# Another order of the first loads and steps, and one inverse in two blocks of 16, in a delta-rule attention with two MLPs

## The chip, the cores and the metric

The kernel runs on one core of a Trainium2 chip. The metric is the device time of one execution in microseconds (us), the median of several runs.

## The reference

The first part is a delta rule per batch and head (4 x 8 of them, 768 steps, head dimension 48). Its output goes through two MLPs, the first with a leaky slope alpha per hidden unit, the second with a gate.

```python
k_n = k / (np.linalg.norm(k, axis=-1, keepdims=True) + 1e-06)
for t in range(S):
    y[:, :, t] = np.einsum('bhd,bhde->bhe', q[:, :, t], state)
    v_old = np.einsum('bhde,bhd->bhe', state, kt)
    state = state + bt[:, :, :, None] * np.einsum('bhd,bhe->bhde', kt, vt - v_old)
...
h = x @ w_in
g = np.maximum(h, 0.0) + alpha * np.minimum(h, 0.0)
x = g @ w_out
...
out = (silu(x @ w_gate) * (x @ w_val)) @ w_out
```

x has 3072 rows of 384; the hidden widths are 2048 and 1536. The results are those of fp32.

## The kernel before, in words

The 768 steps are cut into 24 chunks of 32 steps. Within a chunk the recurrence is solved by the inverse of a lower triangular 32 x 32 matrix, one for each of the 32 pairs of batch and head; four chunks make a window, and the 128 inverses of a window lie on the 128 partitions. For a chunk c the steps are: `pre_T` (line 177) transposes k and q on TensorE, `pre_G` (197) multiplies k with k (part 0) and k with q (part 1) and copies them out, the second one with a mask either on VectorE or, with `raw=True`, copied by ScalarE and masked later on GpSimd by `mask_m` (194); `do_KS`, `do_QS`, `do_U`, `do_S`, `do_Y` and `do_XT` (484 to 574) work with the state, apply the inverse, and put the chunk's output into x1, the input of the first MLP. `scale_v` (449) scales v on GpSimd with norms that come out of the inverse. For the first two chunks `pre_cross` (228) replaces the state.

There are two ways to the inverse. `lanes` (313) eliminates 31 rows on VectorE, with the right-hand columns (from 10 on) on GpSimd. `lanes2` (368) treats two diagonal blocks of 16 side by side, 15 steps on VectorE, and gets the block below the diagonal by two products on TensorE for each half of the lanes: `out1` (line 408) and the one at line 430, 64 matmuls each, after each pair a subtraction on VectorE (439). Both are generators; each `next` issues one step. Before the change `lanes2` serves chunks 0 to 3 and `lanes` the rest.

The weights arrive as 64-bit words and are cut to fp32 pairs: `all_w1` (869) is a generator whose step issues ScalarE's scaling (592), one of three VectorE operations (597, 599, 603) and the subtractions on GpSimd and VectorE (875), and for later slices also loads on ScalarE's queue. `load_w1` brings slices of 384 KB; slices 2j and 2j+1 belong to hidden block j, and slices 10 and 11 are thus needed by the first conversion step of block 5, 12 and 13 by that of block 6. Loading k or q of a window is `load_nat` (101): four loads of 192 KB, one for each batch; the even batches fill `nat[0]`, the odd ones `nat[1]`.

The order of work on every engine is the order of the program, written out by hand: `prelude` (910) first, then a list of events `at(u, ...)` sorted by the column u. A column is one hidden block of the first MLP for two chunks: `H1(n, j)` (675, nine matmuls) at 16n + j, its output split by `H1_parts`, and `O1` (705, nine matmuls) 2.5 columns later. H1's results lie in two PSUM banks, so H1 of a column waits until VectorE has read the one two columns before (line 693). The steps of chunk c stand around `base(c)` = 2.9, 7.7, 22.6, 27.2, then 8(c - 2). The conversion goes on up to column 10.5, the inverse of chunks 4 to 7 runs in 37 steps from column 10.9 to 22.6, and `do_U(4)` that needs it stands at 24.1. After the first MLP the second one runs in much the same way.

A small activation that writes one element of a tile makes a later load into that tile wait for ScalarE to come to it; the kernel does so at line 942 for q and at line 987 for the second use of `nat`.

Of the kernel before, what the change touches and what calls it, by code (L numbers as in the profile page):

```python
# [24 lines left out]
def kernel(  # L25
# [25 lines left out]
    nc = tc.nc  # L51
# [49 lines left out]
    def load_nat(w, nm, to, eng=nc.sync):  # L101

        src = {"k": k, "q": q}[nm]
        for b in range(4):
            eng.dma_start(
                out=to[b % 2][:, :, b // 2, 0:D],
                in_=src[b, :, w * 128:w * 128 + 128, :].rearrange("h t d -> t h d"),
            )
# [515 lines left out]
    def load_w1(*slices, eng=nc.sync):  # L624
        for i in slices:
            load_wide(*w1_src(i), w1_64[i // 2][:, i % 2], eng)
# [280 lines left out]

    CONVS = C_A, C_B, C_C, C_D = (1, 3, 3, 1)

    def prelude():  # L910
        nc.vector.memset(St[:, 0, 0:2, :], 0.0)
        for z in range(2):
            nc.vector.memset(nat[z][:, :, :, D:64], 0.0)
        for z in range(2):
            nc.vector.memset(k2_t[z][:, H * D :], 0.0)
        nc.vector.memset(mask[:, 0:1], 1.0)
        nc.scalar.activation(out=mask[:, 1:2], in_=mask[:, 0:1], func=AF.Sqrt)
        make_identity(nc, ident)
        for z in range(2):
            nc.gpsimd.memset(natq0[z][:, :, :, D:64], 0.0)  # L920
        nc.gpsimd.memset(mask, 1.0)
        for g in range(4):
            m = mask[32 * g:32 * g + 32, :]
            nc.gpsimd.affine_select(
                out=m, in_=m, pattern=[[1, C]], compare_op=ALU.is_gt, fill=0.0, base=0, channel_multiplier=-1
            )
        load_nat(0, "k", nat)
        load_w1(0, 1)
        load_beta(0, nc.gpsimd)
        load_v(0, nc.gpsimd)  # L930
        load_v(1, nc.gpsimd)
        warm(4, St[:, 0, 0:2, :].rearrange("p h e -> p (h e)"))
        n = 0
        for b1 in range(2):
            for half in range(2):
                pre_T(0, "k", b1, half, nat, early=n % 2 == 1, eng="act" if n % 2 == 0 else "dve")
                n += 1
        go(conv, 2)
        for c in range(4):
            pre_G(c, (0,), early=c % 2 == 1)  # L940
            if c == 1:
                nc.scalar.activation(out=natq[0:1, 0, 0, 0, 0:1], in_=mask[0:1, 0:1], func=AF.Copy)
        load_nat(0, "q", natq0)
        load_w1(2, 3, 4)
        load_nat(1, "k", nat)
        nc.sync.dma_start(out=alpha_r, in_=moe_alpha.rearrange("(j p) -> j p", p=128))
        load_k2(0)
        load_w1(*range(5, 10))
        go(conv, C_A)
        inv = lanes2(0, True)  # L950
        go(inv, 3)
        load_beta(1)
        n = 0
        for b1 in range(2):
            for half in range(2):
                pre_T(0, "q", b1, half, natq0, early=n % 2 == 1)
                n += 1
        go(inv, 6)
        pre_G(0, (1,))
        go(inv, 2)  # L960
        pre_G(1, (1,), early=True)
        pre_cross()
        for c in (2, 3):
            pre_G(c, (1,), early=c == 2, raw=True)
        pa = bank(False, "pal")
        nc.tensor.transpose(pa[:, 0:J1], alpha_r, ident[0:J1, 0:J1])

        c = slope[:, 0]
        nc.vector.tensor_scalar(c, pa[:, 0:J1], -1.0, 1.0, op0=ALU.mult, op1=ALU.add)
        nc.vector.tensor_scalar(slope[:, 1], c, 0.0, 2.0, op0=ALU.is_ge, op1=ALU.mult)  # L970
        nc.vector.tensor_scalar(slope[:, 1], slope[:, 1], -1.0, None, op0=ALU.add)
        nc.vector.tensor_tensor(c, c, slope[:, 1], ALU.mult)
        nc.vector.tensor_scalar(c, c, -1.0, None, op0=ALU.mult)
        go(inv, 2)
        scale_v(0)
        scale_v(1)
        mask_m(2)
        mask_m(3)
        for b1 in range(2):
            for half in range(2):  # L980
                pre_T(1, "k", b1, half, nat)
        load_k2(1)
        load_w1(*range(10, 2 * W1_SP))
        warm(6)
        go(inv, 7)
        go(inv)
        nc.scalar.activation(out=nat[0][0:1, 0, 0, 0:1], in_=mask[0:1, 0:1], func=AF.Copy)
        load_nat(1, "q", nat)
        go(conv, C_B)
        go(inv)  # L990
        do_U(0)
        load_v(2)
        go(conv, C_C)
        do_KS(1)
        do_QS(0)
        do_Y(0)
        go(conv, 2)
        do_U(1)
        do_QS(1)
        go(conv, 3)  # L1000
        do_XT(0)
        go(conv, C_D)
        do_Y(1)
        go(conv, 1)
        do_XT(1)
        return inv
# [6 lines left out]
    for i in range(CONV_N):  # L1013
        at(-0.5 + i * CONV_END / CONV_N, go, conv)

    for w in range(1, NWIN):
        P = base(4 * w) - 32
        if w == 1:
# [3 lines left out]
                at(1.8 + 1.05 * z, pre_T, 1, "q", z // 2, z % 2, nat)  # L1022
            for z in range(4):
                at((5.7, 7.0, 8.8, 10.4)[z], pre_G, 4 + z)
            l0, l1, n = 10.9, 22.6, LANES
        else:
            if w < TURN:
                at(P - 5, load_nat, w, "k", nat)
# [121 lines left out]
```

## Time and profile before

| | |
|---|---|
| runs (us) | 1096.22, 1096.61, 1093.04; median 1096.22 |
| profiled execution | 1096.7 us, of it 1094.7 us from the first to the last instruction |
| busy, share of the span | TensorE 96%, VectorE 56%, ScalarE 35%, GpSimd 32% |
| granted TensorE clock | 0.976 in the mean |

In the rows further down, PE is TensorE's matmuls, PEld its weight loads, DVE VectorE, ACT ScalarE, POOL GpSimd, SP the queue that issues most loads; PEclk is the granted TensorE clock, 1.00 being 2.4 GHz and 0.50 being 1.2 GHz. Times count from the start of the span. A square bracket tells how long the engine was idle before and what released it; "issue" is a wait for nothing that the profile shows. An fp32 matmul of the attention part is recorded twice, so the 64 matmuls of a product are 128 records, while H1 and O1 are nine records each. The ends of matmuls are modelled and overlap with the next.

### The profile page before, as it was taken

What the parts mean: (1) busy time and instruction counts of PE and PEld (TensorE: products, weight loads), DVE (VectorE), ACT (ScalarE), POOL (GpSimd) and SP (SyncE); (2) the same over time, 40 slices, a digit from 0 to 9 for tenths busy, and PEclk for the clock granted to TensorE, in tenths of its full rate; (3) what the DMA queues carried; (4) which work ended last, traced back from release to release, by engine and by line L of the source; (5) the groups of instructions that cost most, each with busy time, mean ns of one, the idle gap of its engine ahead of it and who ended that gap; (6) DMA issues with size and microseconds to landing.
All of it is one profiled execution on the core that took longest, in us unless ns stands there. A gap on an engine that the chain in (4) does not pass through costs nothing.

```text
span 1094.7 us, 35682 instructions
## 1 busy us (share of the span) xinstructions
PE 1054.4 (96%) x15661; PEld 969.7 (89%) x15661; DVE 610.8 (56%) x1218; ACT 387.7 (35%) x833; POOL 346.2 (32%) x517
## 2 busy tenths in 40 slices
PE   5688899999999999999999999999999999999998
PEld 5578888999999999999999998888888888888887
DVE  5689974985796598589443453433333333333332
ACT  3356343344334434443444653222122222222211
POOL 4275652843573283266333541201001001010000
PEclk8569999999999999999999999999999999999999
DMA  8674051453345236330341441010010010100001
GB/s 180 179 203 113 10 100 47 71 112 104 68 57 145 67 62 137 90 85 10 118 128 57 153 137 58 1 58 1 1 58 1 16 43 1 58 1 1 29 1 29
DMA packets 165979, 76.34 MB, mean 70 GB/s; under 512 B 129824, under 2 KB 160576, under 8 KB 165824
## 3 DMA queue, kind: packets, MB, share of 16 engines
q1 hardware_dynamic: 160256, 66.28, 24.6%
q10 hardware_dynamic: 5184, 7.37, 2.1%
q8 instruction: 122, 2.00, 0.8%
q0 software_dynamic: 384, 0.41, 0.2%
q14 instruction: 33, 0.27, 0.1%
HBM read 57.52 MB, written 16.52 MB: 68 GB/s over the span
## 4 chain that ended last, share of the span: by engine, by line
PE 91%; DVE 5%; issue 2%; DMA 1%; ACT 1%; SPq 0%; ACTq 0%; DVEq 0%
PE gv L772 27%; PE o L713 19%; PE h L682 18%; PE o L802 14%; PE pst L527 2%; PE pg L207 2%; PE pu L506 2%; PE py L548 2%; PE pk L462 2%; PE py L462 1%; PE pt L185 1%; PE px L570 1%; DVE X L331 1%; DVE tmp L323 1%; DVE w L599 0%
## 5 line engine op out<-in xcount | busy, mean ns | idle before, releaser
L772 PE MATMUL gv<-x2s,w 128*128 128x512 f32 x1296 | 307.6, 391 | 0.0
L772 PEld LDWEIGHTS gv<-x2s,w 128*128 128x128 f32 x1296 | 242.5, 188 | 47.7
L713 PE MATMUL o<-gh,w 128*128 128x256 f32 x1728 | 245.6, 288 | 3.5 <-POOL gh L702 1.8
L682 PE MATMUL h<-xh,w 128*128 128x256 f32 x1152 | 240.7, 285 | 4.0 <-DVE pn L693 2.9
L702 POOL TENSOR_TENSOR gh<-pn,gh 128x256 fp32r<-128x256 f32 x192 | 157.0, 817 | 250.3 <-ACT gh L701 224.3
L713 PEld LDWEIGHTS o<-gh,w 128*128 128x128 f32 x1728 | 217.2, 189 | 9.5 <-POOL gh L702 2.4
L682 PEld LDWEIGHTS h<-xh,w 128*128 128x128 f32 x1152 | 191.4, 190 | 7.3 <-DVE pn L693 4.4
L693 DVE SCALAR_TENSOR_TENSOR pn<-pn,slope,h 128x256 f32<-128x256 f32 x192 | 91.2, 475 | 132.9 <-ACT pn L692 132.8
L682 PE MATMUL h<-xl,w 128*128 128x256 f32 x576 | 162.8, 283 | 0.1
L802 PE MATMUL o<-w,us 128*128 128x384 f32 x864 | 162.5, 337 | 0.0
L802 PEld LDWEIGHTS o<-w,us 128*128 128x128 f32 x864 | 151.9, 188 | 7.1 <-DVE os L815 1.3
L692 ACT ACTIVATE pn<-h,slope 128x256 f32<-128x256 f32 x192 | 90.2, 470 | 139.9 <-PE h L682 139.6
L784 DVE TENSOR_TENSOR sg<-sg,gv 128x512 f32<-128x512 f32 x72 | 49.5, 687 | 152.2 <-ACT sg L782 152.1
L701 ACT ACTIVATE gh<-pn 128x256 fp32r<-128x256 f32 x192 | 79.9, 416 | 142.0 <-DVE pn L693 140.2
L682 PEld LDWEIGHTS h<-xl,w 128*128 128x128 f32 x576 | 109.4, 190 | 0.6 <-DVE xl L574 0.6
L789 ACT ACTIVATE us<-u 128x512 fp32r<-128x512 f32 x72 | 45.5, 632 | 171.1 <-DVE u L785 171.1
L757 POOL TENSOR_TENSOR x2s<-x2r,x2s 128x512 fp32r<-128x512 f32 x15 | 19.3, 1310 | 266.6 <-ACT x2s L755 266.6
L782 ACT ACTIVATE sg<-gv 128x512 f32<-128x512 f32 x72 | 43.0, 597 | 159.4 <-PE gv L772 159.4
L790 DVE TENSOR_TENSOR us<-u,us 128x512 fp32r<-128x512 f32 x72 | 49.9, 693 | 54.5 <-ACT us L789 54.5
L785 DVE TENSOR_TENSOR u<-sg,gv 128x512 f32<-128x512 f32 x72 | 49.5, 687 | 49.3 <-PE gv L772 48.8
L331 DVE TENSOR_TENSOR X<-X,tmp 128x31 f32<-128x31 f32 (+29 forms) x155 | 65.1, 420 | 4.8
L323 DVE TENSOR_TENSOR tmp<-L,X 128x31 f32<-128x31 f32 (+29 forms) x155 | 57.8, 373 | 1.8
(121 smaller groups left out, 970.5 us busy)
## 6 DMA issues: line engine op xcount, KB each, us to landing
w<-in_moe_w_out_dram SPq DMA_DIRECT2D x19, 384.0 KB
wf<-w2d SPq DMA_DIRECT2D x36, 192.0 KB
k<-in_k_dram SPq DMA_DIRECT2D x96, 48.0 KB
x2d<-xs SPq DMA_DIRECT2D x12, 384.0 KB
w<-in_moe_w_gate_dram SPq DMA_DIRECT2D x12, 384.0 KB
w<-in_moe_w_val_dram SPq DMA_DIRECT2D x12, 384.0 KB
x2r<-x2d SPq DMA_DIRECT2D x24, 192.0 KB
v<-in_v_dram SPq DMA_DIRECT2D x88, 48.0 KB
```

The lines of the kernel that those rows point to most:

```text
L323: eng.tensor_tensor(w, t.L[:, i + 1:C, i:i + 1].to_broadcast([128, n, m]), t.X[:, i:i + 1, c0:c0 + m].to_broadcast([128, n, m]), ALU.mult,)
L331: eng.tensor_tensor(Xv, Xv, w, ALU.subtract)
L682: nc.tensor.matmul(ps[:, 0:N1], w[:, a, kk * 128:kk * 128 + 128], x[b][:, kk, :], start=(i == 0), stop=(i == 3 * NK - 1),)
L692: nc.scalar.activation(out=g, in_=hv, func=AF.Relu, scale=slope[:, 0, j:j + 1])
L693: nc.vector.scalar_tensor_tensor(out=g, in0=g, scalar=slope[:, 1, j:j + 1], in1=hv, op0=ALU.mult, op1=ALU.add)
L701: nc.scalar.activation(out=gh[:, 0], in_=g, func=AF.Copy)
L702: nc.gpsimd.tensor_tensor(gh[:, 1], g, gh[:, 0], ALU.subtract)
L713: nc.tensor.matmul(o[:, dm // 2, (dm % 2) * N1:(dm % 2) * N1 + N1], w[:, a, dm * 128:dm * 128 + 128], g[:, b], start=(j == 0 and i == 0 an ...
L772: nc.tensor.matmul(p[:, 0:N2], w2[j, z][:, a, kk * 128:kk * 128 + 128], x[:, b, kk], start=(i == 0), stop=(i == 3 * NK - 1),)
L784: nc.vector.tensor_tensor(sg, sg, ps[0], ALU.mult)
L790: nc.vector.tensor_tensor(us[:, 1], u, us[:, 0], ALU.subtract)
L802: nc.tensor.matmul(o2_t[n][t][:, 0:DM], us[:, a, t * 128:t * 128 + 128], w[:, b, :], start=(j == 0 and i == 0), stop=(j == J2 - 1 and i == 2),
```

## The change

The prelude is put into another order. The four loads of `load_nat` go in the order of batches 0, 2, 1, 3. SP's first loads become q of window 0, k of window 1, alpha, w1 slices 2 to 5, k of chunk 0, w1 slices 6 to 9, k of chunk 1; slices 10 and 11 wait for a mark behind the first product of the inverse, and q of window 1, slices 12 and 13 and v of chunk 2 for one behind `do_Y(0)`. The steps of the first inverse go on without other VectorE work between them: the masks of chunks 0 and 1 go to GpSimd behind the 17 steps, as does `scale_v`; alpha is copied by ScalarE, and the slopes are worked out behind `do_XT(0)`. The six warm matmuls are gone. `pre_G` of chunks 2 and 3 and their masks leave the prelude for columns 4.3 to 10.2. The inverse of chunks 4 to 7 is made by `lanes2`: 21 steps from column 10.9 at a distance of 0.33 and four from 19.4 at a distance of 0.7, so that the four products stand at 17.5, 19.4, 20.1 and 20.8.

```diff
     def load_nat(w, nm, to, eng=nc.sync):
...
-        for b in range(4):
+        for b in BS:
...
+    def mark(a):
+        nc.scalar.activation(out=a, in_=mask[0:1, 0:1], func=AF.Copy)
...
         load_nat(0, "q", natq0)
-        load_w1(2, 3, 4)
         load_nat(1, "k", nat)
         nc.sync.dma_start(out=alpha_r, in_=moe_alpha.rearrange("(j p) -> j p", p=128))
+        load_w1(*range(2, 6))
         load_k2(0)
-        load_w1(*range(5, 10))
+        load_w1(*range(6, 10))
+        load_k2(1)
...
-        go(inv, 6)
-        pre_G(0, (1,))
-        go(inv, 2)
-        pre_G(1, (1,), early=True)
+        pre_G(0, (1,), raw=True)
+        pre_G(1, (1,), early=True, raw=True)
         pre_cross()
-        for c in (2, 3):
-            pre_G(c, (1,), early=c == 2, raw=True)
-        pa = bank(False, "pal")
+        pa = bank(True, "pal")
         nc.tensor.transpose(pa[:, 0:J1], alpha_r, ident[0:J1, 0:J1])
...
+        nc.scalar.activation(out=slope[:, 1], in_=pa[:, 0:J1], func=AF.Copy)
         for b1 in range(2):
             for half in range(2):
                 pre_T(1, "k", b1, half, nat)
-        load_k2(1)
-        load_w1(*range(10, 2 * W1_SP))
-        warm(6)
-        go(inv, 7)
+        go(inv, 17)
+        for c in range(2):
+            scale_v(c)
+        for c in range(2):
+            mask_m(c)
         go(inv)
-        nc.scalar.activation(out=nat[0][0:1, 0, 0, 0:1], in_=mask[0:1, 0:1], func=AF.Copy)
-        load_nat(1, "q", nat)
+        mark(w1_64[5].rearrange("p a n -> p (a n)").bitcast(F32)[0:1, 0:1])
+        load_w1(10, 11)
         go(conv, C_B)
         go(inv)
         do_U(0)
-        load_v(2)
         go(conv, C_C)
         do_KS(1)
         do_QS(0)
         do_Y(0)
+        mark(nat[0][0:1, 0, 0, 0:1])
+        load_nat(1, "q", nat)
+        load_w1(*range(12, 2 * W1_SP))
+        load_v(2)
         go(conv, 2)
...
         do_XT(0)
+        c = slope[:, 0]
+        nc.vector.tensor_scalar(c, slope[:, 1], -1.0, 1.0, op0=ALU.mult, op1=ALU.add)
...
+    def step1(box):
+        if not box:
+            box.append(lanes2(1))
+        go(box[0])
...
-            l0, l1, n = 10.9, 22.6, LANES
+            for z in range(2):
+                at((4.3, 9.6)[z], lambda z=z: pre_G(2 + z, (1,), raw=True))
+                at((4.9, 10.2)[z], mask_m, 2 + z)
+            n = 0
+            box1 = []
+            for z in range(LANES2 - 4):
+                at(10.9 + 0.33 * z, step1, box1)
+            for z in range(4):
+                at(19.4 + 0.7 * z, step1, box1)
```

## Rows read from the trace of the kernel before

**Rows 1.** The stages: stretch, busy us of each engine (records), PEclk, DMA share, GB/s

```profile
0.00:60.60 60.60, 36.80 (x1291) 32.90 (x1291) 37.19 (x85) 24.28 (x52) 25.06 (x40) 0.68 0.74 176
...
91.30:116.80 25.50, 22.66 (x677) 20.34 (x676) 24.75 (x34) 13.51 (x26) 14.25 (x12) 1.00 0.30 77
116.80:149.40 32.60, 27.79 (x269) 25.21 (x267) 30.64 (x81) 10.85 (x32) 24.77 (x54) 1.00 0.23 46
...
200.00:1094.70 894.70, 889.42 (x11324) 818.76 (x11322) 462.73 (x918) 299.89 (x636) 244.76 (x373) 1.00 0.23 59
```

**Rows 2.** TensorE in order of time, prelude: start us, us, line, tiles, records [idle before]

```profile
25.93 0.53 PE L235 MATMUL pg<-kqt 48*32 48x64 f32 x10 [2.61 <-issue]
...
38.05 1.53 PE L408 MATMUL pi<-TT,GL 32*32 32x16 f32 x128 [2.06 <-DVE TT L273]
...
44.80 0.83 PE L430 MATMUL pi<-tmp,Dm 16*32 16x16 f32 x44 [3.34 <-issue]
46.14 1.50 PE L506 MATMUL pu<-v,TT 32*32 32x48 f32 x64 [0.51 <-DVE TT L439]
...
60.62 0.58 PE L682 MATMUL h<-xh,w 128*128 128x256 f32 x1 [1.07 <-ACT xh L573]
```

**Rows 3.** VectorE in order of time, prelude

```profile
20.21 0.20 DVE L392 TENSOR_TENSOR tmp<-L,X 128x30 f32<-128x30 f32 x1
...
23.01 0.78 DVE L392 TENSOR_TENSOR tmp<-L,X 128x110 f32<-128x110 f32 x1
...
30.98 0.17 DVE L969 TENSOR_SCALAR slope<-pal 128x16 f32<-128x16 f32 x1 [5.05 <-PE pal L966]
...
36.95 1.05 DVE L273 STREAM_TRANSPOSE TT<-X 128x512 f32<-128x512 f32 x1
...
60.60 0.56 DVE L574 TENSOR_TENSOR xl<-px,xh 128x384 fp32r<-128x384 f32 x1 [0.65 <-ACT xh L573]
```

**Rows 4.** VectorE groups, 19.4 to 37 us: busy us, mean ns, idle before

```profile
L394 DVE TENSOR_TENSOR X<-X,tmp 128x30 f32<-128x30 f32 (+7 forms) x15 | 4.4, 293 | 0.4
```

**Rows 5.** Matmul records from the start up to a stop (x)

```profile
0.00:98.70 98.70, 71.70 (x2260) 0.74 0.74 186
0.00:103.99 103.99, 75.33 (x2388) 0.75 0.71 178
```

**Rows 6.** TensorE in order of time, 93 to 105 us

```profile
94.98 0.97 PE L207 MATMUL pg<-kqt 48*32 48x64 f32 x51 [0.82 <-issue]
...
100.36 0.85 PE L713 MATMUL o<-gh,w 128*128 128x256 f32 x5 [1.65 <-issue]
...
104.36 0.37 PE L462 MATMUL py<-St,kqt 48*32 48x48 f32 x14 [0.37 <-issue]
```

**Rows 7.** SP, TensorE and ScalarE in order of time: loads and who reads them

```profile
12.60 2.65 SPq L105 DMA_DIRECT2D natq<-in_q_dram  x4
...
17.19 3.81 PE L185 MATMUL pt<-ident,natq 128*128 128x128 f32 x16 [1.92 <-DMA natq<-in_q_dram]
...
58.49 0.91 ACT L592 ACTIVATE w<-w 128x768 f32<-128x768 f32 x1
```

**Rows 8.** H1's matmuls (line 682) in columns 11 to 21: stretch, busy us (records)

```profile
113.80:149.36 35.56, 14.33 (x99) 12.29 (x100) 1.00 0.20 42
```

**Rows 9.** TensorE in order of time, in the loop

```profile
69.03 1.42 PE L408 MATMUL pi<-TT,GL 32*32 32x16 f32 x128
...
89.14 1.10 PE L207 MATMUL pg<-kqt 48*32 48x64 f32 x64
...
143.14 1.31 PE L713 MATMUL o<-gh,w 128*128 128x256 f32 x9
...
145.36 0.60 PE L185 MATMUL pt<-ident,nat 128*128 128x128 f32 x4
```

**Rows 10.** VectorE groups, 116 to 156 us

```profile
L331 DVE TENSOR_TENSOR X<-X,tmp 128x60 f32<-128x60 f32 (+29 forms) x31 | 12.4, 401 | 1.0
```

More of the change, by code (lines that the diff above doesn't have):

```diff
@@ L941, in prelude @@
             if c == 1:
-                nc.scalar.activation(out=natq[0:1, 0, 0, 0, 0:1], in_=mask[0:1, 0:1], func=AF.Copy)
+                mark(natq[0:1, 0, 0, 0, 0:1])
         load_nat(0, "q", natq0)
-        load_w1(2, 3, 4)
         load_nat(1, "k", nat)
         nc.sync.dma_start(out=alpha_r, in_=moe_alpha.rearrange("(j p) -> j p", p=128))
+        load_w1(*range(2, 6))
         load_k2(0)
-        load_w1(*range(5, 10))
+        load_w1(*range(6, 10))
+        load_k2(1)
         go(conv, C_A)
@@ L957, in prelude @@
                 n += 1
-        go(inv, 6)
-        pre_G(0, (1,))
-        go(inv, 2)
-        pre_G(1, (1,), early=True)
+        pre_G(0, (1,), raw=True)
+        pre_G(1, (1,), early=True, raw=True)
         pre_cross()
-        for c in (2, 3):
-            pre_G(c, (1,), early=c == 2, raw=True)
-        pa = bank(False, "pal")
+        pa = bank(True, "pal")
         nc.tensor.transpose(pa[:, 0:J1], alpha_r, ident[0:J1, 0:J1])
[L968 to L978, printed above, removed]
+        nc.scalar.activation(out=slope[:, 1], in_=pa[:, 0:J1], func=AF.Copy)
         for b1 in range(2):
@@ L1001, in prelude @@
         do_XT(0)
+        c = slope[:, 0]
+        nc.vector.tensor_scalar(c, slope[:, 1], -1.0, 1.0, op0=ALU.mult, op1=ALU.add)
+        nc.vector.tensor_scalar(slope[:, 1], c, 0.0, 2.0, op0=ALU.is_ge, op1=ALU.mult)
+        nc.vector.tensor_scalar(slope[:, 1], slope[:, 1], -1.0, None, op0=ALU.add)
+        nc.vector.tensor_tensor(c, c, slope[:, 1], ALU.mult)
+        nc.vector.tensor_scalar(c, c, -1.0, None, op0=ALU.mult)
         go(conv, C_D)
```

## The prediction

> **What bounds the kernel now.** I read the stages first [rows 1]. From 200 us to the end TensorE is busy 889.4 of 894.7 us at full clock, so a change of the first 200 us passes to the end one for one, unless it adds or removes TensorE work. Before 60.6 us TensorE works 36.8 us, at a mean clock of 0.68: this is the prelude, and what ends it is a chain of waits. Between 116.8 and 149.4 us it works 27.8 of 32.6 us while VectorE is busy 30.6: there the elimination of chunks 4 to 7 holds it. Between 91.3 and 116.8 us VectorE is busy 24.8 of 25.5: the weight conversion holds it.
>
> Next, TensorE in the prelude [rows 2]: the products of the first inverse start at 38.05, the second product stops for 3.34 us that nothing in the profile explains ("issue"), `do_U(0)` starts at 46.14 and the first H1 at 60.62. Then VectorE [rows 3, 4]: the elimination starts at 20.21, stands still for 5.05 us until the transpose of alpha is done, works off the slopes, and ends at 36.95. Its 30 instructions, 15 on X as in [rows 4] and 15 on tmp (4.2 us), are busy 8.6 us of these 16.7.
>
> The "issue" stops have a pattern [rows 5, 6]. Two of them fall after 2260 and 2388 matmul records, 128 apart, in the middle of groups whose data are there. So every 128 records (a small fp32 matmul counts as two) there is a border, and from border 2260, left at 100.36, to the release of 2388 at 104.36 it took 4.0 us. I read this as a supply of instructions in blocks: 128 records of small matmuls last about 1.4 us, of H1 and O1 some 15 us (18 records in 2.22), so only crowds of small matmuls can outrun it.
>
> **The change, term by term**, against the profiled execution's 1096.7 us.
>
> *A, up to do_U(0).* The new order of the four loads of k (0, 2, 1, 3) lets the first transposes start after two loads instead of three; q, at 17.19, waits 4.5 us after the first issue for three of its four [rows 7]. With about 1.1 us per load I take 1.0 us for all that follows (0 if the fourth load or ScalarE's sqrt sets the pace, 1.5 at best). The slopes leave the elimination, the two masks go to GpSimd, and scale_v comes after it: in its time one VectorE step took 0.78 us where the mean is 0.29 [rows 3, 4]. Left are 8.6 us of work and 0.7 of gaps, less some 0.5 of that slowdown: 8.9 us for 16.74, so −7.85. The first product starts at 38.05 − 1.0 − 7.85 = 29.2. TensorE must be free by then: the cross products, at 25.93 behind a border [rows 2], end 1.0 earlier near 25.5; alpha and the 16 transposes of k, like q's 3.8 us at half clock [rows 7], follow: 29.3. It is just free. The stretch from this product to do_U(0) was 8.1 us with the 3.34 us stop. The border there now waits 1.7 us by 4.2 us per block, as w1 slices 10 to 13 no longer load beside it; then the subtraction also has three conversion steps ahead of it on VectorE. I take 6.6, so −1.5. Sum A: −10.3 (−7 if TensorE comes 2 us late and the stop stays; −11 at best).
>
> *B, do_U(0) to the first H1:* 14.5 us before. VectorE now works off the slopes (five small instructions from 30.98, about 1.3 us) behind do_XT(0), and it was idle only 0.65 us before the last xl [rows 3]: +0.7. Slices 12 and 13 of w1 now wait, on SP's queue, behind four loads of q that start only with the mark behind do_Y(0). The mark comes near 41.7. The four q loads went out in 2.65 us and three of them were in 4.5 us after the first issue [rows 7]; the fourth and 0.77 MB of weights bring this to about 8 us, 49.7. ScalarE needs the slices for the conversion that stood at 58.49, 12.35 us behind do_U(0) [rows 7]; that is 48.2 now. Behind that instruction on ScalarE's queue stands the copy that H1 waits for. +1.3 (0 to 3, as ScalarE's own weight loads share the engines). Queued behind them on SP is v of chunk 2; its reader comes over 10 us later, free. alpha and k2(1) are on SP ahead of their readers, free. ScalarE gets five more small copies (two G, alpha, two marks); it is busy 24.3 of 60.6 us [rows 1], which hides them, and without that cover they cost some 1.5. Sum B: +2.0; the first H1 comes 8.3 us earlier, at 52.3.
>
> *C, in the loop, columns 0 to 11.* G of chunks 2 and 3 (64 records each) come out of the prelude. One such group takes 1.1 us [rows 9] (at 89.14), half a border comes with it. At column 4.3 TensorE has no slack: +1.6. At 9.6 VectorE sets the pace: +0.5 (0 to 1.6). Their masks, two GpSimd steps, slow VectorE's conversion: +0.3 (0 to 0.8). Sum C: +2.4. The six warm matmuls that go stood in idle time: nothing, unless they kept the clock up; it fell again before the second product.
>
> *D, the inverse.* Columns 11 to 22 (99 H1 records) last 35.6 us [rows 8]. O1 and H1 of a column take 2.22 us [rows 9] (143.14 to 145.36), eleven columns 24.4; with S and Y (64 records each, priced like the G at 89.14) 2.0, and with 19 full-width records of XT and four transposes at 0.12 another 2.3, that is 28.7. So 6.9 us are lost to VectorE, more than the 4.8 idle of [rows 1], since pipelined tails count as busy. VectorE's elimination there takes 23.1 us in 31 steps (12.4 on X as in [rows 10], 10.7 on tmp), 0.75 a step and 3.16 steps a column, beside pn. Two blocks take 15 steps of about 0.59: three a column and pn make 2.2 us, just TensorE's pace. The three transposes, 3 us, fall near column 17.3, where the new product gives cover. −6.5 (−4.8 to −6.9). TensorE gets four products of 128 records, 1.42 us each with the changeover [rows 9] (at 69.03): +5.7 (6.5 at half clock). These 512 records bring four borders; the products at 19.4, 20.1 and 20.8 stand 0.7 columns (1.6 us) apart, so 128 records pass in 2.7 us and the supply needs 4.0 [rows 6]: 1.1 to 1.3 us short at two of them, none at the others. +2.2 (0 to 8). Sum D: +1.4.
>
> Sum: −10.3 + 2.0 + 2.4 + 1.4 = −4.5, so 1092.2. The profiled execution lies 0.5 us above the median of the runs (1096.2), so I forecast 1091.7 for the median. Where the clock rises behind the first H1 shifts with its start; nine H1 records take 2.2 us instead of 1.1 at half clock, so 1.5 either way for that.
>
> A rule speaks to the last term of D. The Trainium skill (Runtime: NRT & Kernel Launch, "Instruction fetch mechanics") says that instructions come in 16 KiB blocks of 256 and that crossing into the next is mostly hidden. The trace agrees on the size (128 records, each a weight load and a matmul) and disagrees on hidden wherever small matmuls crowd. By that rule D would be −0.8 and the whole about 1089.
>
> **The rivals.**
> *1. Borders are mostly free* (the page's rule): 2.2 us less in D and 0.5 in C, 1089.0. For it: most borders in the trace pass without a stop. Against it: the stops of [rows 6]. 0.12.
> *2. The prelude gives only 6.* If the loads of w1 slices 12 and 13 take 3 us too long, or TensorE reaches the products 2 us late, A and B make −5.5 instead of −8.3 and the whole ends at 1094.5: no change. For it: TensorE is free only just in time, and ScalarE's queue is strict. Against it: fewer bytes compete. 0.25.
> *3. Slower: the products starve.* Between column 17.5 and do_QS(4) at 22.95 some 760 records pass, six blocks. At the 5.4 us from one release at 94.98 to the next at 100.36 [rows 6] they need 32 us where the work takes 21: 11 us instead of 2.2, so 1100.5. It decides from about 5 us a block. For it: the q loads of chunks 8 to 11 and the weight loads run there. Against it: the very next block took 4.0, and DMA is light there (0.23 before 149.4 [rows 1]). 0.15.
> The change does what it says: the order of each engine is written out by hand, so I give no chance to its not being carried out.
>
> **How the numbers follow.** Forecast and what lies close, 1088.5 to 1094.5: 0.48; rivals as above. Faster by over 0.3% (under 1092.9; 0.3% is about what a measurement of this kernel can tell): 0.42 of the forecast and rival 1, 0.54. Within 0.3%: rival 2 and 0.05 of the forecast, 0.30. Slower: rival 3 and rest, 0.16. The range takes in rival 1 with its best A and rival 2 with half a clock slip, and stops short of rival 3: 1086.5 to 1098.
>
> **What would show it.** Right: VectorE's 30 elimination steps without a stop of 5 us, first product near 29, do_U(0) near 36, first H1 near 52; on ScalarE a wait of 1 to 2 us on w1 near 48; no pn wait on TensorE in columns 13 to 20, and "issue" stops of about 1 us within the products of columns 20 and 21. Wrong: a first H1 after 55, stops of 2 us or more in the products, or VectorE still the pace between columns 13 and 20.

## The result and the profile after

The changed kernel took 1102.91 us (median of six runs, 1102.21 to 1105.6) against 1096.23 for the kernel before beside it. The measured ratio, which is not the quotient of these two medians, is 1.0073, interval 1.0059 to 1.0087. By the medians it is slower by 6.7 us, where 4.5 less were forecast; the range ended at 1098.0. The profiled execution spans 1101.4 us (1094.7 before). All executions of a kernel here lie within about one per cent of its median, but for one of run 9's ten, of 1725 us, which its ratio leaves out.

First the stages of the kernel after, as in [rows 1] and [rows 8] (stretch, busy us of each engine with its records, PEclk, DMA share, GB/s; the last row of H1's matmuls alone, columns 11 to 21):

```profile
0.00:58.40 58.40, 34.11 (x1152) 29.61 (x1152) 35.75 (x83) 23.99 (x54) 24.23 (x40) 0.67 0.79 184
...
116.80:149.40 32.60, 26.68 (x597) 25.52 (x584) 21.31 (x61) 10.67 (x29) 8.24 (x12) 0.95 0.18 39
...
200.00:1101.40 901.40, 896.30 (x11438) 825.68 (x11436) 468.53 (x941) 303.22 (x644) 249.03 (x381) 1.00 0.23 59
...
111.56:156.92 45.36, 15.30 (x99) 13.66 (x100) 0.92 0.23 51
```

From 116.8 to 149.4 us VectorE is busy 21.3 us where it was 30.6: the relief is there. TensorE is busy 1.1 us less than before, though it has more to do. H1's columns 11 to 21 last 45.4 us where they lasted 35.6, at a mean clock of 0.92. The loss sits here: the first H1 still starts 2.2 us earlier than before, column 28 starts 7.5 us later, and what follows is as long as it was (921.9 us, 922.6 before).

TensorE of the kernel after in order of time, in the prelude, against [rows 2]:

```profile
26.91 0.58 PE L235 MATMUL pg<-kqt 48*32 48x64 f32 x11 [2.98 <-issue]
...
30.87 0.99 PE L408 MATMUL pi<-TT,GL 32*32 32x16 f32 x97
33.57 0.47 PE L408 MATMUL pi<-TT,GL 32*32 32x16 f32 x31 [1.70 <-issue]
34.56 1.48 PE L430 MATMUL pi<-tmp,Dm 16*32 16x16 f32 x97 [0.53 <-issue]
38.15 0.62 PE L430 MATMUL pi<-tmp,Dm 16*32 16x16 f32 x31 [2.10 <-issue]
39.35 1.50 PE L506 MATMUL pu<-v,TT 32*32 32x48 f32 x64 [0.58 <-POOL w L875]
...
58.37 0.58 PE L682 MATMUL h<-xh,w 128*128 128x256 f32 x1 [2.81 <-ACT xh L573]
```

The first product starts 7.2 us earlier, do_U(0) 6.8 and the first H1 2.25. Next VectorE, against [rows 3]: the elimination runs from 20.18 to 28.94, 8.76 us without the stop of 5 us.

```profile
20.18 0.20 DVE L392 TENSOR_TENSOR tmp<-L,X 128x30 f32<-128x30 f32 x1
...
28.94 1.09 DVE L273 STREAM_TRANSPOSE TT<-X 128x512 f32<-128x512 f32 x1
```

ScalarE in order of time (ACTq is its own queue for loads), with SP's loads of q:

```profile
45.45 2.72 SPq L105 DMA_DIRECT2D nat<-in_q_dram  x4
48.22 2.14 SPq L608 DMA_DIRECT2D w<-in_moe_w_in_dram  x1
...
53.65 0.36 ACTq L608 DMA_DIRECT2D w<-in_moe_w_out_dram  x1
54.11 0.49 ACT L557 ACTIVATE ys<-py 128x384 f32<-128x384 f32 x1 [4.02 <-DMA nat<-in_q_dram]
56.28 0.88 ACT L592 ACTIVATE w<-w 128x768 f32<-128x768 f32 x1 [1.69 <-DMA w<-in_moe_w_out_dram]
```

ScalarE stands 4.02 us for a load of q that it does not read: in the trace the fourth load of q, issued at 47.40, and ScalarE's weight load of 53.65, the instruction ahead, complete on the same semaphore, number 101, and the weight load waits for it. Then it stands 1.69 us for the weights. The copy that H1 waits for is behind both.

TensorE in the loop, columns 17 to 21, against [rows 9], then VectorE at the same place:

```profile
135.41 1.43 PE L408 MATMUL pi<-TT,GL 32*32 32x16 f32 x128 [4.16 <-DVE TT L273]
136.77 2.29 PE L713 MATMUL o<-gh,w 128*128 128x256 f32 x9
...
148.71 0.59 PE L408 MATMUL pi<-TT,GL 32*32 32x16 f32 x48 [0.95 <-issue]
...
152.53 0.70 PE L430 MATMUL pi<-tmp,Dm 16*32 16x16 f32 x62 [0.91 <-issue]
...
155.15 1.94 PE L713 MATMUL o<-gh,w 128*128 128x256 f32 x9
```

```profile
133.71 0.19 DVE L394 TENSOR_TENSOR X<-X,tmp 128x30 f32<-128x30 f32 x1
133.81 0.47 DVE L693 SCALAR_TENSOR_TENSOR pn<-pn,slope,h 128x256 f32<-128x256 f32 x1
134.21 1.05 DVE L273 STREAM_TRANSPOSE TT<-X 128x512 f32<-128x512 f32 x1
```

The first product, at column 17.5 in TensorE's order, stands 4.16 us for VectorE, whose elimination ends only at 133.9. Behind it O1 takes 2.29 us instead of 1.3, and again behind the stops of the last product (1.94). The stages say what the clock was:

```profile
131.00:135.40 4.40, 0.25 (x3) 0.04 (x2) 4.16 (x13) 1.78 (x5) 1.84 (x3) 1.00 0.00 2
135.40:138.80 3.40, 3.39 (x137) 3.36 (x138) 1.65 (x2) 0.39 (x1) 0.15 (x1) 0.62 0.02 5
...
150.80:157.00 6.20, 5.29 (x149) 5.09 (x148) 0.90 (x2) 0.98 (x3) 1.54 (x3) 0.72 0.74 160
```

### The profile page after: what moved, and what is told of

Read it like the earlier page. It is cut to its first block, busy times and chain, and to the rows that moved or that the text cites. A ratio compares the mean times of both kernels' runs of the same rounds, so it can differ in the third digit from the quotient of the medians.

```text
span 1101.4 us, 36626 instructions
## 1 busy us (share of the span) xinstructions
PE 1059.1 (96%) x16161; PEld 975.1 (89%) x16161; DVE 596.3 (54%) x1186; ACT 389.5 (35%) x839; POOL 331.9 (30%) x478
## 4 chain that ended last, share of the span: by engine, by line
PE 90%; DVE 5%; issue 2%; DMA 1%; SPq 1%; ACT 0%; POOL 0%; ACTq 0%; POOLq 0%; DVEq 0%
PE gv L772 27%; PE o L713 19%; PE h L682 18%; PE o L802 14%; PE pst L527 2%; PE pg L207 2%; PE pu L506 2%; PE py L548 2%; PE pk L462 2%; PE py L462 1%; PE pt L185 1%; DVE X L394 1%; DVE tmp L392 1%; PE px L570 1%; DVE w L599 1%
## 5 line engine op out<-in xcount | busy, mean ns | idle before, releaser
L785 DVE TENSOR_TENSOR u<-sg,gv 128x512 f32<-128x512 f32 x72 | 49.5, 687 | 49.7 <-PE gv L772 48.8
L331 DVE TENSOR_TENSOR X<-X,tmp 128x60 f32<-128x60 f32 (+29 forms) x124 | 52.6, 424 | 3.9
L323 DVE TENSOR_TENSOR tmp<-L,X 128x60 f32<-128x60 f32 (+29 forms) x124 | 46.8, 377 | 1.2
```

Of the source, the lines that this page charges most:

```text
L331: eng.tensor_tensor(Xv, Xv, w, ALU.subtract)
L785: nc.vector.tensor_tensor(u, sg, ps[1], ALU.mult)
```

## The experiments

The table has the median of each run, its ratio to the kernel before beside it, and from TensorE's rows the start of do_U(0) and of H1 in columns 0, 11 and 28.

| run | us | ratio, interval | do_U(0) | col. 0 | col. 11 | col. 28 |
|---|---|---|---|---|---|---|
| before | 1096.23 | | 46.14 | 60.62 | 113.80 | 172.06 |
| after | 1102.91 | 1.0073, 1.0059 to 1.0087 | 39.35 | 58.37 | 111.56 | 179.51 |
| 1 prelude only | 1095.31 | 0.9999, 0.9987 to 1.0011 | 38.94 | 58.28 | 112.87 | 171.58 |
| 2 inverse only | 1103.64 | 1.0072, 1.0055 to 1.0088 | 46.75 | 60.63 | 110.32 | 180.96 |
| 3 first product late | 1101.95 | 1.0061, 1.0041 to 1.0080 | 39.34 | 58.72 | 111.65 | 177.18 |
| 4 loads early | 1102.65 | 1.0070, 1.0051 to 1.0089 | 38.93 | 56.96 | 112.88 | 182.09 |
| 5 no products | 1091.81 | 0.9962, 0.9947 to 0.9976 | 38.57 | 58.33 | 111.05 | 167.76 |
| 6 products apart | 1100.91 | 1.0046, 1.0032 to 1.0060 | 41.51 | 60.97 | 115.27 | 177.66 |
| 7 q last | 1096.20 | 1.0003, 0.9992 to 1.0014 | 38.44 | 56.13 | 112.80 | 171.41 |
| 8 G in idle time | 1094.17 | 0.9988, 0.9975 to 1.0000 | 39.01 | 58.73 | 111.12 | 171.77 |
| 9 weights late | 1102.45 | 1.0051, 1.0031 to 1.0072 | 37.15 | 56.30 | 109.11 | 175.40 |
| 10 loads in turn | 1102.18 | 1.0061, 1.0039 to 1.0082 | 39.45 | 59.12 | 112.98 | 178.81 |
| 11 warm | 1094.64 | 0.9982, 0.9966 to 0.9999 | 38.30 | 58.08 | 109.84 | 170.83 |
| 12 longer elimination | 1094.21 | 0.9980, 0.9964 to 0.9997 | 39.67 | 59.07 | 109.47 | 171.43 |
| 13 masks early | 1094.47 | 0.9976, 0.9962 to 0.9991 | 38.53 | 57.58 | 107.04 | 167.87 |
| 14 all three | 1096.10 | 0.9988, 0.9973 to 1.0003 | 38.85 | 58.69 | 109.93 | 170.93 |
| 15 masks early, weights late | 1094.87 | 0.9994, 0.9983 to 1.0005 | 37.30 | 58.37 | 110.48 | 170.96 |

One profile's columns 0 to 10 differ by 1.6 to 3.5 us between kernels that are alike up to there (after and runs 3, 5 and 6: 52.7 to 54.3; run 2 and before: 49.7 and 53.2), so single profiles are compared column by column and totals by the medians. A profile can also lie off its kernel's median: run 13's was the fastest of its twelve executions (1090.5 us), run 9's the fastest of its ten (1099.1).

**Runs 1 and 2: each half of the change alone.**

```diff
-            n = 0
-            box1 = []
-            for z in range(LANES2 - 4):
-                at(10.9 + 0.33 * z, step1, box1)
-            for z in range(4):
-                at(19.4 + 0.7 * z, step1, box1)
+            l0, l1, n = 10.9, 22.6, LANES
```

Run 1 is the kernel after with this; run 2 is the kernel before with the reverse.

> The changed kernel with the inverse of chunks 4 to 7 put back to the 37 elimination steps of before; prelude and G of chunks 2 and 3 as changed. Theory (the loss sits in the inverse's products, columns 16 to 22, where the changed kernel is 9.9 us longer than the one before; the prelude still gains 2.2): first H1 at 58.4, columns 16 to 22 in about 20.3 us as before, the whole 1093.5 to 1094.5, faster than before by 2 us. Rival (the new prelude moves the loop into a worse position of instruction borders and clock, whatever inverse runs): columns 16 to 22 stay over 25 us and the whole stays above 1098.

> The kernel before with only the inverse of chunks 4 to 7 in two blocks, at the same columns as in the changed kernel. Theory: columns 16 to 22 in about 30 us against 20.3, a wait of about 4 us of TensorE for VectorE's transpose ahead of the first product, the whole 1104 to 1106, slower than the changed kernel by its prelude's 2 us. Rival (the inverse costs only its product work, 5.6 us, less VectorE's relief): 1097 to 1099.

The inverse alone costs what the whole change costs (1.0072), and the new prelude alone changes nothing (0.9999): I had expected some 2 us of gain to be left, and run 2 to be slower than the kernel after by as much. So the loss is the inverse's own, and it does not come from the earlier prelude: run 2 has the same wait (TensorE's waits from 110 to 180 us: who waited for whom, us in total, times, longest).

```profile
PE pi L408 <- DVE TT L273: 4.2, 1, 4.2
```

**Run 3: the first product at 19.4 instead of 17.5.**

```diff
-            for z in range(LANES2 - 4):
+            for z in range(LANES2 - 5):
                 at(10.9 + 0.33 * z, step1, box1)
-            for z in range(4):
+            for z in range(5):
                 at(19.4 + 0.7 * z, step1, box1)
```

> The changed kernel with the first of the four products moved from column 17.5 to 19.4, and the other three, 0.7 columns apart, behind it (20.1, 20.8, 21.5). Theory: VectorE comes to the transpose that the first product reads about 4 us after TensorE stands there; two columns later it is there, so the wait of 4.2 us goes, and with it the half clock behind it (about 1.5 us). The whole 1096.5 to 1098. Rival (the wait moves with the product, or the products' own work and borders are the loss): gain under 2 us, 1101 or more.

The wait is gone and the total all but stays: a miss for my theory, and the rival's 1101 or more. TensorE of run 3 in order of time:

```profile
145.97 0.69 PE L408 MATMUL pi<-TT,GL 32*32 32x16 f32 x60 [0.47 <-issue]
...
150.25 1.15 PE L430 MATMUL pi<-tmp,Dm 16*32 16x16 f32 x69 [1.73 <-issue]
151.32 2.29 PE L713 MATMUL o<-gh,w 128*128 128x256 f32 x9
```

With the products closer to each other a block's border stops one for 1.73 us, and O1 behind it runs at half clock again. Taking the wait away moves part of its cost into stops; the rest must be in the products themselves. Runs 5 and 6 price them.

**Run 5: no products; run 6: products 1.3 columns apart.**

```diff
             ps[z] = bank(early, "pi")
+            if w == 1:
+                nc.tensor.matmul(ps[z][:, 0:N], ident, G[:, 0:HC, 0:HC], start=True, stop=True)
+                return
```

Run 5 is run 3 with this and the same for the second product: it leaves the products out and puts one wide matmul in the place of each. Run 6 is run 3 with

```diff
-                at(19.4 + 0.7 * z, step1, box1)
+                at((18.6, 19.9, 21.2, 22.5, 23.0)[z], step1, box1)
```

> The third run's kernel (first product at column 19.4), in which the four small products of the second inverse (512 small matmuls, 1024 records) are left out: one wide matmul fills each of the four halves of a PSUM bank in their place, so the output is not the reference's. It prices the small products with their borders and the half clock behind them against the third run, and the relief of VectorE alone against the first run. Theory (the products cost about 5.2 us of work, 2.2 of stops and some 2 of half clock; the relief of VectorE is smaller than the 6.5 us I counted, near 3.5): 1093 to 1094.5, columns 16 to 22 in 17 to 19 us. Rival (the relief is the whole 6.5 us, so the products cost 12): 1089 to 1091. Second rival (there is no relief, TensorE had the time anyway): 1095 to 1097.

> The kernel after, with the twenty steps up to the end of the elimination as they are and the four products at columns 18.6, 19.9, 21.2 and 22.5, 1.3 columns (2.9 us) apart instead of 0.7. Theory (supply: a block of 128 records takes about 4 us, so products that stand closer stop, and the stops pull the clock down): the stops within the products go, the clock stays up to column 22, 1097 to 1099. Rival (the products cost their work and break the clock wherever they stand, since 16x16 matmuls leave most of TensorE empty): 1101 to 1103, H1 at half clock behind each product.

Run 5 is 10.1 us faster than run 3 and 3.5 faster than run 1, better than my theory's 1093, short of the rival's whole relief. In run 6 the clock stays at 1.00 in every stretch from column 16 to 28, as the theory had it, and yet the total is 1100.9, above its 1097 to 1099. Columns 16 to 27 of run 6, then of run 5 (stages), and what run 6 waits for in order of time on TensorE:

```profile
130.42:177.66 47.24, 43.62 (x1275) 41.20 (x1275) 20.54 (x47) 19.40 (x52) 12.54 (x17) 1.00 0.33 74
```

```profile
126.18:167.76 41.58, 39.84 (x772) 37.67 (x772) 20.41 (x47) 19.44 (x52) 12.57 (x17) 1.00 0.37 83
```

```profile
139.16 1.25 PE L408 MATMUL pi<-TT,GL 32*32 32x16 f32 x128 [1.49 <-DVE TT L273]
...
153.87 0.93 PE L430 MATMUL pi<-tmp,Dm 16*32 16x16 f32 x88 [0.66 <-issue]
...
157.60 0.57 PE L462 MATMUL pk<-St,kqt 48*32 48x48 f32 x33 [1.08 <-issue]
```

The 5.66 us between the two are, but for 0.2, four products at 1.2 (4.8, less 1.2 for run 5's four wide matmuls) and 3.6 us in which TensorE is idle, against 1.7 in run 5. So with full clock and hardly a stop the products still cost their work, and that work alone is about what VectorE's relief is worth. The medians of the two runs differ by 9.1 us, 3.4 more than these columns show; for that no stage gives a cause.

**Runs 4, 7 and 10: the loads.** Run 4 is the kernel after with

```diff
-        load_w1(10, 11)
+        load_w1(*range(10, 2 * W1_SP))
+        mark(nat[0][0:1, 0, 0, 0:1])
+        load_nat(1, "q", nat)
...
-        mark(nat[0][0:1, 0, 0, 0:1])
-        load_nat(1, "q", nat)
-        load_w1(*range(12, 2 * W1_SP))
```

Run 7 is run 1 with the longer `load_w1` of this edit, and with the mark and the load of q behind do_XT(1) instead. Run 10 is the kernel after with the old order of the loads:

```diff
-        for b in BS:
+        for b in range(4):
             eng.dma_start(
```

> The changed kernel with q of window 1 and w1 slices 12 and 13 loaded behind slices 10 and 11, ahead of do_U(0), as before the change. Theory (ScalarE stands 4.0 us in its own weight load, which waits until a load of q has landed, and 1.7 us for slices 12 and 13): both waits go; the first H1 comes at 53 to 55 instead of 58.4, the whole 1098 to 1100. Rival (the heavier loads ahead of do_U(0) hold up TensorE's instruction blocks there): do_U(0) comes 2 us or more later and the first H1 still after 57.

> The first run's kernel (prelude of the kernel after, inverse of the second window as before), with w1 slices 12 and 13 loaded right behind slices 10 and 11, and the four loads of q for chunks 4 to 7 moved to the end of the prelude, so that no q load shares a completion semaphore with ScalarE's own weight load. Theory (ScalarE's stand of 4 us in the kernel after came from the q loads issued just ahead): ScalarE no longer waits, first H1 near 55, 1092.5 to 1094.5 if the columns behind keep their pace. Rival (as in the fourth run, what ScalarE wins is lost to slower instruction blocks under the weight loads): first H1 at 57 or later, 1095 to 1096.

> The kernel after with the four loads of k and q of each window in their old order 0, 1, 2, 3. I had counted 1.0 us for the new order. Theory (the second half of the transposes waits for the fourth load at 7.7 us in either order, so the order is worth nothing): do_U(0) at 38.5 to 40, 1102 to 1104, no difference from the kernel after. Rival (the order gives its 1.0 us, hidden by a block's border that fell elsewhere): do_U(0) one later, near 40.3, 1103.5 to 1105.

In run 4 both waits of ScalarE are gone, and the first H1 comes only 1.4 us earlier, as the stops in TensorE's small matmuls grew: neither the theory's 53 to 55 nor the rival's later do_U(0). In run 7 the first H1 starts at 56.1, near the theory, but column 11 at 112.8, as in run 1, and the total is that of before: a miss for the theory, and not by its rival's way. Its gain is gone by column 3 (74.30; 74.11 in run 1): ScalarE now stands 4.16 us at 67.19 for a load of k, and in the columns 0 to 2 TensorE is busy 17.4 of 18.2 us at a mean clock of 0.53. Run 10 cannot be told from the kernel after: the order of the loads is worth nothing that these runs can tell.

**Run 9: fewer bytes beside the products.**

```diff
         load_k2(0)
-        load_w1(*range(6, 10))
         load_k2(1)
...
-        mark(w1_64[5].rearrange("p a n -> p (a n)").bitcast(F32)[0:1, 0:1])
-        load_w1(10, 11)
         go(conv, C_B)
         go(inv)
+        for z in (3, 4, 5):
+            mark(w1_64[z].rearrange("p a n -> p (a n)").bitcast(F32)[0:1, 0:1])
+        load_w1(*range(6, 12))
         do_U(0)
```

> The kernel after with w1 slices 6 to 11 loaded only behind the second product of the first inverse, just ahead of do_U(0), so that few bytes move while the elimination's last part and the two products run. Read in the prelude alone: do_U(0) at 38.4 to 41.5 us in the seven profiles with the order of after, with 4.3 us of stops inside the first two products in the kernel after. Theory (an instruction block takes longer to come while the weights load): the stops in the two products fall to 1.5 to 2.5 us, do_U(0) near 36.5 to 37.5; the weights then come late, first H1 at 58 or later, total 1102 to 1105. Rival (a block takes its 4 us whatever the loads do): stops of 4 us again, do_U(0) at 38.5 to 40.

Stages from 28 to 38 us (the last numbers are clock, DMA share and GB/s) of the kernel after, of run 4 and of run 9:

```profile
28.00:38.00 10.00, 5.81 (x241) 5.38 (x239) 6.23 (x10) 5.64 (x15) 4.52 (x6) 0.67 0.68 202
```

```profile
28.00:38.00 10.00, 4.16 (x250) 3.50 (x252) 5.33 (x6) 4.32 (x10) 5.69 (x7) 0.67 0.74 196
```

```profile
28.00:38.00 10.00, 7.36 (x315) 6.79 (x317) 7.21 (x11) 5.75 (x17) 5.72 (x7) 0.67 0.20 39
```

The stops in the first two products sum to 4.33 us at a DMA share of 0.68, 5.74 at 0.74 and 1.79 at 0.20. TensorE of run 4, then of run 9, their longest:

```profile
37.73 0.62 PE L430 MATMUL pi<-tmp,Dm 16*32 16x16 f32 x31 [3.21 <-issue]
```

```profile
35.69 0.62 PE L430 MATMUL pi<-tmp,Dm 16*32 16x16 f32 x31 [1.25 <-issue]
```

Same product, same 97 records ahead of the border: the instruction block comes later while the weights load. How much later does not go by the share alone: in the thirteen profiles that load these weights here, at shares of 0.61 to 0.74, the stops sum to anything from 3.2 to 6.4 us. do_U(0) came as the theory had it, the first H1 earlier (56.3, where 58 or later was expected). That a prelude 2 us shorter moves the total little (1102.45) belongs to the next group.

**Runs 8, 11 to 15: where the prelude's gain goes.** Run 8 is run 1 with G of chunks 2 and 3 behind the prelude's last transposes; run 13 adds their masks:

```diff
-            for z in range(2):
-                at((4.3, 9.6)[z], lambda z=z: pre_G(2 + z, (1,), raw=True))
-                at((4.9, 10.2)[z], mask_m, 2 + z)
...
         do_XT(1)
+        for c in (2, 3):
+            pre_G(c, (1,), early=c == 2, raw=True)
+        for c in (2, 3):
+            mask_m(c)
```

Runs 11 and 12 are run 8 with the first and the second of these; run 14 is run 13 with both, and run 15 is run 13 with run 9's edit.

```diff
         do_Y(1)
+        warm(8)
...
             pre_G(c, (1,), early=c == 2, raw=True)
+        warm(4)
```

```diff
-            l0, l1, n = 10.9, 22.6, LANES
+            l0, l1, n = 10.9, 23.4, LANES
```

> The first run's kernel with G of chunks 2 and 3 issued behind the last transposes of the prelude, where TensorE waits 2.8 us for ScalarE, instead of at columns 4.3 and 9.6. It prices part C of the change. Theory (each group costs 1.1 us of work and half a border in the loop): columns 0 to 11 shorter by about 2.4 us, first H1 later by at most 0.5, 1093 to 1094. Rival (TensorE had slack in columns 0 to 11, since the weight conversion on VectorE paces them): no change, 1095 to 1096.

> The eighth run's kernel (prelude of after, inverse as before, G of chunks 2 and 3 behind the prelude) with 12 wide matmuls without use set into TensorE's idle time before the first H1: eight behind do_Y(1), four behind G. In all profiles so far the columns 0 to 3 begin at half clock and H1 of column 6 starts at 88.5 to 90.7 us whether the first H1 starts at 56.1 or at 60.6 (one at 93.1). Theory (what an earlier first H1 wins is lost since the clock then rises no earlier): with TensorE kept busy the clock is up by the first or second column, column 6 starts near 86.5, 1091 to 1092.5. Rival (the conversion of the weights and its loads pace the columns up to 9): the clock rises earlier, TensorE waits more, column 9 as before, 1093.5 to 1095.

> The eighth run's kernel with the steps of the second window's elimination (as before, without products) spread over columns 10.9 to 23.4 instead of 22.6, to see whether VectorE's relief is to be had by spreading alone. Theory (VectorE is short by some 3 us in these columns, and 0.8 column more gives it 1.8): 1092.5 to 1093.8. Rival (the inverse is then late for do_U(4) at column 24.1 and TensorE waits there): 1094.5 to 1097.

> The eighth run's kernel with the masks of chunks 2 and 3 on GpSimd right behind their G at the end of the prelude, instead of at columns 4.9 and 10.2. In the eighth run do_Y(3) stood 3.28 us at 117.96 for GpSimd's second mask, which sits behind the last conversion step on GpSimd's queue. Theory (this wait is what C's move still cost, and the prelude's gain was lost there): the wait goes, H1 of column 14 near 122 instead of 124.9, 1091 to 1092.5. Rival (VectorE's conversion, whose last step ended at 116.3 with G moved as without, paces these columns): the wait goes and pn waits and waits for U take its place, 1093.5 to 1094.5.

> The thirteenth run's kernel with the 12 wide matmuls of the eleventh run and the elimination spread to column 23.4 as in the twelfth, the parts that were not slower each, together. Theory: 1090.5 to 1092.5. Rival (they draw on the same slack): 1093 to 1094.5.

> The thirteenth run's kernel with w1 slices 6 to 11 loaded behind the second product of the first inverse, as in the ninth run. Theory (a block of instructions comes sooner while few bytes move, which brought do_U(0) to 37.2 and the first H1 to 56.3 there): do_U(0) at 36.5 to 37.5, 1091.5 to 1093.5. Rival (VectorE's conversion paces the columns up to 14, so what the prelude wins is lost there, as in the first, seventh and eleventh run): do_U(0) as early, 1094 to 1095.5, no better than the thirteenth run.

Run 8's columns 0 to 11 are 2.2 us shorter than run 1's, as the theory had it, but the columns 11 to 15 are 2.4 longer. TensorE of run 8, column 12:

```profile
117.96 1.39 PE L548 MATMUL py<-U,mt 32*32 32x48 f32 x64 [3.28 <-POOL mt L195]
```

do_Y(3) waits for the mask that the change moved from the prelude to column 10.2, where it comes behind the weight conversion on GpSimd. This wait is in the kernel after too, 1.24 us. Run 13 removes it; in its place H1 of column 14 waits for VectorE:

```profile
118.92 0.39 PE L682 MATMUL h<-xh,w 128*128 128x256 f32 x1 [1.64 <-DVE pn L693]
```

From run 1 to run 13 the ratio falls by 0.0023: about 2.5 us, with some 2 of uncertainty, are the price of G and masks in the columns (1.8 by the medians). Run 11 warms TensorE and the columns 0 to 2 take 13.1 us instead of 14.5, but the total is run 8's: its stages from column 0 to 2 and in column 3:

```profile
58.08:71.15 13.07, 12.26 (x428) 11.14 (x429) 10.93 (x14) 7.94 (x17) 8.77 (x7) 0.85 0.65 181
71.15:81.33 10.18, 6.22 (x154) 5.70 (x152) 9.27 (x10) 3.99 (x8) 8.98 (x8) 0.83 0.89 247
```

In column 3 VectorE is busy 9.3 and GpSimd 9.0 of 10.2 us, most of it with the conversion, but TensorE does not stand for them. Its idle time there is two stops for nothing that the profile shows, at a DMA share of 0.89:

```profile
75.29 0.89 PE L462 MATMUL pk<-St,kqt 48*32 48x48 f32 x52 [2.55 <-issue]
...
80.97 0.60 PE L185 MATMUL pt<-ident,nat 128*128 128x128 f32 x4 [1.41 <-issue]
```

Columns 6 to 13 of run 1:

```profile
90.65:123.09 32.44, 30.05 (x861) 27.61 (x855) 31.13 (x47) 16.01 (x35) 17.66 (x16) 1.00 0.18 55
```

VectorE is busy 31.1 of 32.4 us. These columns take 32.0 to 33.0 us in all kernels but run 13 (34.5, with the wait above) and runs 8, 11 and 12 (35.1 to 37.2, with the wait for the mask). So what is won up to column 6 mostly reaches column 14: against before 3.6 and 3.8 us in run 9, 5.8 and 4.2 in run 13. The first H1's gain is lost ahead of that. Column 6 starts at 90.17 after 60.62 (before) and at 90.26 after 56.13 (run 7). Columns 0 to 5 of before, of run 7 and of run 13:

```profile
60.62:90.17 29.55, 27.18 (x747) 25.26 (x747) 25.06 (x30) 16.95 (x34) 19.88 (x16) 0.79 0.67 190
```

```profile
56.13:90.26 34.13, 31.23 (x810) 28.77 (x810) 25.05 (x31) 17.93 (x36) 20.29 (x17) 0.70 0.80 198
```

```profile
57.58:84.41 26.83, 24.17 (x747) 22.19 (x747) 24.17 (x27) 17.09 (x35) 23.75 (x18) 0.91 0.76 202
```

VectorE's work is nearly the same in the three, and TensorE is busy most of the time; what differs is the granted clock (run 7 also has one G more here). Over all the profiles these columns are longest at the lowest clock (33.4 and 34.1 us at 0.70, runs 4 and 7) and shortest at the highest (28.0 and 26.8 at 0.91, runs 12 and 13), with a loose order between.

So the times that the rivals of runs 11, 13 and 15 gave came, but their cause, VectorE's conversion, is seen only in the 1.6 to 1.9 us that TensorE waits for pn in columns 11 to 15 of runs 13 and 15. For run 7 the trace speaks for the clock, the theory of run 11, and no run shows it by itself: run 11 raised the clock of these columns only from run 8's 0.81 to 0.88, won 1.0 us in them, and its total is run 8's. Run 15's do_U(0) came at 37.3, as its theory had it, and its first H1 no earlier than without (58.37). Run 12 can't be told from run 8. Run 14, the two together, is above its theory and its rival (1096.10), and why stays open. Runs 8 and 11 to 13 end with ratios of 0.9976 to 0.9988, run 13 lowest, with intervals that end at 0.9991 to 1.0000; run 15, which differs from run 13 in its loads alone, is back at 0.9994. So the prelude without the products, G and masks in the columns is worth 0.1 to 0.2% at best.

## Why the prediction was wrong

Against the forecast of 1091.7 the kernel is 11.2 us slower. The two steps that failed are **the sum of D** (+1.4 forecast; about +8 by the ratios of after and run 1) and **the sum of A and B** (-8.3 forecast; the first H1 came 2.25 us earlier, and about 2.5 show in the total by run 13, in which part C is taken out and the inverse is as before). By the stages of the profiles the first H1 is 6.1 us later than forecast, the columns 0 to 10 are 2.4 shorter, the columns 11 to 27 are 8.3 longer and the rest is 0.8 shorter. C was sized rightly as far as the runs can tell: 2.4, measured about 2.5 with some 2 of uncertainty.

*D.* The columns 11 to 27 took 58.26 us before and 67.95 after, 9.7 more. TensorE's waits of the kernel before from 110 to 180 us (who waited for whom, us in total, times, longest):

```profile
PE h L682 <- DVE pn L693: 2.9, 5, 1.6
PE o L713 <- POOL gh L702: 1.8, 3, 1.0
```

Term by term:
- Relief, -6.5 forecast. Run 5 gives it alone: 56.71, less 1.2 for its four wide matmuls, so -2.8 by the columns against before; by the medians of runs 1 and 5 (3.5 and the same 1.2) -4.7. The forecast got its 6.9 us of loss by subtraction and gave nearly all of it to VectorE's elimination; the waits above are 4.7, and of these 2.9 for VectorE's pn. In run 5 waits for pn and xs are left, and the conversion of the weights still ends inside these columns.
- Products, +5.7 forecast: from start to next start 5.3. Right.
- Borders, +2.2 forecast: 0.95 and 0.91, inside the products of columns 20 and 21 as foretold. Right.
- A wait for the first product: 4.16 us, not in the sum at all. This is the overlooked step. The forecast put the product at column 17.5 "where the new product gives cover" and priced it as work; but it reads the transpose that ends VectorE's elimination, and TensorE's order is fixed. The elimination was costed at 2.2 us of VectorE a column, "just TensorE's pace", with no slack, and it begins behind a conversion whose last step starts at 114.2, inside column 11.
- Half clock: nothing in the sum. O1 at 136.77 takes 1.0 us more than at full clock, H1 and O1 from 153.16 to 156.92 1.4 more, H1 at 138.86 0.3: 2.7. It comes behind TensorE's idle time, and in run 6, without long idle time, not at all.

These make 9.3 to 11.2, against 9.7. Runs 3 and 6 show that placing mends only the wait and the clock: the products cost TensorE 4.8 us at best and the relief is 3 to 5, so even well placed this change of the inverse had next to nothing to win in these columns.

*A.* Forecast do_U(0) at 35.8, measured 39.35. The elimination is right (8.9 forecast, 8.76). The load order is worth 0 instead of 1.0 (the elimination starts at 20.18, 20.21 before; run 10). TensorE "is just free" was 0.9 us late: it ends the transposes of k at 30.95 behind a stop of 2.98. The stretch from product to do_U(0) took 8.5 us instead of 6.6: I had argued that the border stops less because fewer weights load beside it, with slices 10 to 13 gone; but slices 6 to 11 load there, the stops sum to 4.3 us, and run 9, in which they load later, has 1.8.

*B.* Forecast 16.5 from do_U(0) to the first H1, measured 19.0. The wait for slices 12 and 13 is there with 1.69 (1.3 forecast, though 49.7 against 48.2 makes 1.5). The slopes, forecast at 0.7, cost nothing: VectorE stands 4.05 us ahead of the last xl. The 4.02 us of ScalarE's own weight load behind a semaphore of q's load were not in the sum: I had counted bytes on the queues, and not that a later load can wait for an earlier one's completion. What they cost in the total is not shown: in run 7 they are gone there, but ScalarE stands 4.2 us for a load of k ahead of column 3 instead.

*Passing on.* I took the first H1's gain as passed on one for one. What was shown for that, in [rows 1], holds from 200 us on. Between the kernels before and after it did hold to column 11 (2.25 us at the first H1, 2.24 there). In run 7 it did not: of 4.5 us at the first H1 1.1 are left at column 3 and none at column 6. For a clock that rises at another place the prediction allowed 1.5 us either way; columns 0 to 5 took 26.8 us at a mean clock of 0.91 and 34.1 at 0.70. What keeps the clock down there, no run shows.

The rivals: rival 3 had the right sign and nearly the size (1100.5), but not the mechanism. Its blocks of 5.4 us would have stopped the products for 11 us; the stops are 1.9. Rival 2's ScalarE and late TensorE both came; A and B fell short by 6.1 us, where it had 2.8. Rival 1, mostly hidden borders, fails where small matmuls crowd, with stops of up to 3.75 us (run 6, in the prelude's second product); in the wide matmuls of the loop most blocks do pass unseen (from 200 us on 11438 records and 5.1 us of idle time). That a crossing is mostly hidden is what the Trainium skill says (Runtime: NRT & Kernel Launch, "Instruction fetch mechanics"). All three signs named for "wrong" came: a first H1 after 55, a stop of over 2 us in a product (2.10, in the prelude), and VectorE as the pace between columns 13 and 20, with the wait of 4.16.

## What to carry to other kernels

Price an instruction that moves to another engine's fixed order by when its operand is ready on the engine that makes it, and not by its own duration: here that was 4.2 us of wait and then half the clock for what followed. When work moves from one engine to another, compare the measured relief with the added work first; a kernel that leaves the added work out (run 5) gives it in one run. Follow time that is won early through every stage behind it, with the clock of each: run 7 won 4.5 us at the first H1 and had none of it six columns later.

## What was not expected of the hardware

- The stops at instruction blocks' borders depend on what else moves. In the first two products they sum to 1.79 us at a DMA share of 0.20 (run 9) and 2.42 at 0.31 (run 15), from 28 to 38 us; in the other profiles with the new prelude, at 0.61 to 0.74, to 3.2 to 6.4, and among these the share does not give the order (6.39 at 0.68 in run 6, 3.46 at 0.69 in run 7).
- ScalarE stood 4.02 us for a load that it neither issued nor reads, because its own next load was to use the same completion semaphore (number 101). In run 7, with q moved, ScalarE stands 4.2 us at another place, for a load of k; its weight load and that load share number 116.
- The clock fell to half behind 4.2 us of TensorE's idle time and behind two stops of 0.9 us in products (after), and around a stop of 1.73 us in run 3 (0.50 from 149.2 to 156.0); it did not fall behind those of run 6 (1.49, 0.66 and 1.08 us, several columns apart).
